# Two weight loads ahead of an activation tile in the one load ring of a fused mixer and MLP

## The chip, the cores and the metric

The kernel runs on one core of one Trainium2 chip. The metric is the device time of one execution in microseconds (us). Three runs of the kernel before gave 135.13, 135.42 and 135.43, a median of 135.42.

A core has five engines that run side by side: TensorE (PE in the profile; PEld is its weight loads), VectorE (DVE), ScalarE (ACT), GpSimd (POOL) and SyncE (SP), which here only issues DMAs. Each takes its instructions strictly in the order in which they were written for it; an instruction that waits for a semaphore holds up all that stand behind it on the same engine.

## The reference

```python
# x: 1 x 2048 x 512; w1, w2: 512 x 512; w3: 512 x 1792; w4: 1792 x 512; all bf16
def reference(x, w1, w2, w3, w4):
    B, S, D = x.shape
    h = _gelu(_layernorm(x, axis=-1) @ w1)
    c = D // 4
    g0 = jnp.pad(h[:, :, 0*c:1*c], ((0, 0), (1, 0), (0, 0)))[:, :S, :]
    g1 = jnp.pad(h[:, :, 1*c:2*c], ((0, 0), (0, 1), (0, 0)))[:, 1:, :]
    g2 = jnp.pad(h[:, :, 2*c:3*c], ((0, 0), (2, 0), (0, 0)))[:, :S, :]
    g3 = jnp.pad(h[:, :, 3*c:   ], ((0, 0), (0, 2), (0, 0)))[:, 2:, :]
    hs = jnp.concatenate([g0, g1, g2, g3], axis=-1) @ w2
    x1 = x + hs
    h2 = _gelu(_layernorm(x1, axis=-1) @ w3) @ w4
    return x1 + h2
```

The first layer normalizes each row of x, multiplies by w1, applies gelu, shifts the four quarters of the columns by +1, -1, +2 and -2 rows, multiplies by w2 and adds x. The second normalizes the rows of x1, multiplies by w3, applies gelu, multiplies by w4 and adds x1.

## The kernel before

The 2048 rows are cut into 16 tiles of 128 rows. Everything stays in SBUF: x, x1, the weights, and the transposed activations. The work is a list of named operations (`Op`), each with its engine, what it reads and writes, and an assumed duration.

Of tile t in the first layer there are, in the order of the data:

- the load of x (`dma_x...`, L384), some tiles alone, some two or three in one DMA;
- the statistics: on VectorE `bnst` (L432) and `bnag` (L434), or for the tiles in `STAT_ACT` (0, 5, 7, 9, 10, 12 in the first layer) `sum` (L411) and `ssq` (L416) on ScalarE followed by the short `msq` (L424) and `vpe` (L428) on VectorE;
- `rstd` on GpSimd (L439), a power of -0.5 that takes about 0.55 us;
- `norm`: on VectorE (L461), on ScalarE (L470) or GpSimd (L473), as `NORM` says; the last two read `nmr` (L466) as well. Tile 0 is an exception (`NAT`, `SPLIT`): `norm0_0` and `norm0_1` (L448) only subtract the mean, in two halves, and rstd0 is applied later, in gelur0;
- the transposition `tp` on TensorE (L506), copied from PSUM to SBUF by `ev` on VectorE or ScalarE (L514), `both` meaning a half on each (`ev1act` and `ev1dve`); later tiles are transposed by DMA instead (L479, issued by SP);
- the product with w1: `up1` (L642), and for tile 0 `rows0` (L544) in two halves, the first needing w1a and ev0_0, the second w1b and ev0_1; then gelu on ScalarE (L657; for tile 0 gelur0, L585). Tile 0's result is then transposed back by `th0` (L610) and copied by `evh0` on VectorE (L620);
- the product with w2, `mix` (L697), which reads the shifted columns of h of this tile and its neighbours, and `x1` on VectorE (L709, L713), which adds x.

The second layer repeats statistics, norm and transposition on x1, then `up2` (L642) with gelu (L657), `down` (L731), `res` (L739) and the store.

What sets the order:

- TensorE's order is written out by hand, in `SCRIPT`. Its beginning is `warm:9 sa:0 sb:0 ty:1 ra:0 rb:0 ty:2 up1:1 th:0 up1:2 mix:0 ty:3 mix:1`: nine matmuls of zeros (L756), tile 0 transposed in two halves, tile 1 transposed, rows0 in two halves, tile 2 transposed, up1 of tile 1, and so on.
- All loads go through one DMA ring, issued by SP in the order of the list `LOADS`. An item `w1a` is the first half of w1 (rows 0 to 255, 256 KB), `w1b` the second; `x2` is one tile (128 KB), `x0-1` two tiles in one DMA. Items `tp...` in this list only place DMA transposes among the loads; those of tiles that TensorE transposes (tile 2 among them) are ignored.
- The order on VectorE, ScalarE and GpSimd comes from the kernel's own planner when the program is built (`Program.order` and `Program.place`). It assumes a duration for every operation, a due time derived from TensorE's list, and a model of the ring; it then takes on each engine the operation that is ready and has the earliest due time (with a look ahead of 300 ns on VectorE and ScalarE). `BIAS` shifts a few due times by hand. So an edit of `LOADS` changes the assumed arrival times and may reorder any of these engines.

```python
LOADS = """
x0-1 x2 tp2 w1a w1b x3 x4-5 w2b w2a tp5 x6 tp6 x7 x8-10 tp4 w3 x12-13 tp0 x11 tp17 x14-15 tp26 tp5 w4a tp3
w4b
"""
```

`emit` writes the instructions in the planned order and adds the semaphore waits that the reads and writes need.

Of the kernel before, what the change touches and what calls it, by code (L numbers as in the profile page):

```python
# [283 lines left out]
HEV = {0: "dve", 1: "dve", 2: "dve", 3: "dve", 4: "dve", 5: "dve", 6: "dve"}  # L284
BIAS = {"bnag16": -989.166, "nmr10": 207.118, "rstd14": 756.261, "rstd5": 886.138, "ssq1": -15, "ssq15": 1115, "ssq22": -1014, "sum31": 1299.7, "x1_8": 100}
LOADS = """
x0-1 x2 tp2 w1a w1b x3 x4-5 w2b w2a tp5 x6 tp6 x7 x8-10 tp4 w3 x12-13 tp0 x11 tp17 x14-15 tp26 tp5 w4a tp3
w4b
"""
SCRIPT = """  # L290
# [618 lines left out]
```

## Time and profile before

| | |
|---|---|
| median of three runs | 135.42 us |
| span of the profiled execution, first to last instruction | 133.7 us |
| what the median has beyond that span | 1.7 us |
| TensorE busy in the span | 130.6 us (98%) |
| VectorE, ScalarE, GpSimd busy | 50.9, 56.0 and 30.9 us |
| granted TensorE clock | 1.000 |
| HBM read, written | 6.82 MB, 2.10 MB |

The profile is of one execution. Its times count from the first instruction. In the timeline a row is start, length, engine, line, operation, tiles and shapes, with the idle time of the engine before it and what ended that in square brackets. Matmuls are pipelined, and their ends are modelled: two rows that overlap by 0.16 us stand back to back, and the distance of their starts is the better measure. In the chain each row is start, length, and what the time went to. In the rows of windows the columns are the window, its length, the busy time of PE, PEld, DVE, ACT and POOL with the number of instructions, the granted clock, the share of the DMA engines and GB/s. Some matmul records are missing: where a group of four shows three and a gap of one matmul, nothing waited.

The names of single operations (bnst2, norm1, ...) are not in the profile; they follow from the order in which the operations of a line stand on their engine.

### The profile page before, as it was taken

The page shows a single profiled execution, that of the slowest core. Times are in us where ns is not written, and L with a number is a line of the kernel's source. Part 1 is how long each engine was busy: PE and PEld are TensorE (multiplying, and loading weights), DVE is VectorE, ACT ScalarE, POOL GpSimd, SP SyncE. Part 2 cuts the span into 40 slices and gives each one's busy share as a digit, 9 for nine tenths or more (in the row PEclk, how much of TensorE's full clock was granted, in tenths as well). Part 3 has the DMA queues.
Part 4 walks back from the last instruction along what each step waited for, and adds up shares of the span by engine and source line. Part 5 has one row for each costly group of instructions (what it writes and reads, how often), then busy time and mean ns, then how long its engine had stood idle before and what let it go on. Part 6 is the DMA issues. An engine that isn't in the chain of part 4 may idle for free.

```text
span 133.7 us, 2004 instructions
## 1 busy us (share of the span) xinstructions
PE 130.6 (98%) x776; PEld 71.8 (54%) x789; DVE 50.9 (38%) x138; ACT 56.0 (42%) x89; POOL 30.9 (23%) x69
## 2 busy tenths in 40 slices
PE   8999999999999999999999999999999999999994
PEld 3488768874488444444444444444444444444464
DVE  1899998887550830052260003322220000232223
ACT  5699998858657155520025553000006663000000
POOL 2447567696544120012022003100000000000000
PEclk9999999999999999999999999999999999999999
DMA  4999966745442991002211000311111000111112
GB/s 134 329 349 401 237 150 95 83 89 107 98 99 49 295 329 40 0 0 43 77 42 39 0 0 0 78 39 44 39 42 37 0 0 0 39 44 39 39 39 78
DMA packets 21305, 12.19 MB, mean 91 GB/s; under 512 B 13872, under 2 KB 20784, under 8 KB 21296
## 3 DMA queue, kind: packets, MB, share of 16 engines
q1 hardware_dynamic: 20864, 11.93, 32.7%
q10 hardware_dynamic: 432, 0.13, 0.4%
q8 instruction: 6, 0.10, 0.3%
q14 instruction: 3, 0.02, 0.1%
HBM read 6.82 MB, written 2.10 MB: 67 GB/s over the span
## 4 chain that ended last, share of the span: by engine, by line
PE 94%; DMA 2%; DVE 2%; issue 1%; SPq 0%
PE y_ps L642 46%; PE o_ps L731 36%; PE o_ps L697 10%; DMA x_sb<-in_x_dram 2%; PE y_ps L506 1%; DVE st L432 1%; PE y_ps L544 1%; DVE xn_buf L448 0%; DVE xn_buf L461 0%; DVE o_sb L739 0%; PE o_ps L610 0%; DVE mv L434 0%; SPq L894 0%
## 5 line engine op out<-in xcount | busy, mean ns | idle before, releaser
L642 PE MATMUL y_ps<-xnT,w_sb 128*128 128x512 bf16 (+2 forms) x421 | 63.6, 308 | 0.2
L642 PEld LDWEIGHTS y_ps<-xnT,w_sb 128*128 128x128 bf16 x424 | 38.4, 98 | 24.6 <-DVE mv L434 0.2
L731 PE MATMUL o_ps<-w_sb,h2T 128*128 128x512 bf16 (+3 forms) x248 | 48.7, 355 | 0.2
L657 ACT ACTIVATE h2T<-y_ps 128x1024 bf16<-128x1024 f32 (+1 forms) x29 | 28.6, 993 | 47.2 <-PE y_ps L642 47.1
L731 PEld LDWEIGHTS o_ps<-w_sb,h2T 128*128 128x128 bf16 x252 | 23.6, 98 | 25.2
L739 DVE TENSOR_TENSOR o_sb<-o_ps,x_sb 128x512 bf16<-128x512 f32 (+3 forms) x18 | 11.4, 632 | 45.7 <-PE o_ps L731 45.7
L439 POOL TENSOR_TENSOR rstd<-mv,neghalf 128x1 f32<-128x1 f32 x20 | 11.1, 553 | 35.1 <-DVE mv L434 30.1
L697 PE MATMUL o_ps<-w_sb,hT 128*128 128x512 bf16 x58 | 14.8, 379 | 0.3
L432 DVE BATCH_NORM_STATS2 st<-x_sb 128x6 f32<-128x512 bf16 x20 | 13.5, 676 | 2.6 <-DMA x_sb<-in_x_dram 2.5
L713 DVE TENSOR_TENSOR x_sb<-o_ps,x_sb 128x512 bf16<-128x512 f32 x10 | 6.8, 677 | 14.8 <-PE o_ps L697 14.8
L439 POOL TENSOR_TENSOR rstd<-vpe,neghalf 128x1 f32<-128x1 f32 x12 | 6.7, 558 | 15.6 <-DVE vpe L428 15.5
L473 POOL TENSOR_SCALAR xn_buf<-x_sb,rstd,nmr 128x512 bf16<-128x512 bf16 x12 | 9.2, 764 | 1.0 <-DVE nmr L466 0.4
L657 ACT ACTIVATE hT<-y_ps 128x512 bf16<-128x512 f32 (+1 forms) x10 | 8.1, 806 | 3.1 <-PE y_ps L642 2.9
L697 PEld LDWEIGHTS o_ps<-w_sb,hT 128*128 128x128 bf16 x64 | 6.1, 98 | 5.7
L709 DVE SCALAR_TENSOR_TENSOR x_sb<-o_ps,x_sb 128x512 bf16<-128x512 f32 x6 | 4.1, 681 | 12.1 <-PE o_ps L697 12.1
L416 ACT ACTIVATE junk<-x_sb 128x512 bf16<-128x512 bf16 x12 | 7.5, 622 | 2.1 <-DVE x_sb L709 2.0
L461 DVE TENSOR_SCALAR xn_buf<-x_sb,mv,rstd 128x512 bf16<-128x512 bf16 x13 | 6.1, 471 | 2.7 <-POOL rstd L439 2.0
L470 ACT ACTIVATE xn_buf<-x_sb,nmr,rstd 128x512 bf16<-128x512 bf16 x6 | 4.9, 813 | 0.5 <-POOL nmr L466 0.4
L756 PE MATMUL o_ps<-zeros 128*128 128x512 bf16 x9 | 4.0, 631 | 0.4 <-DVE zeros L363 0.4
L411 ACT ACTIVATE junk<-x_sb 128x512 bf16<-128x512 bf16 x6 | 3.7, 624 | 1.2 <-DMA x_sb<-in_x_dram 1.2
L434 DVE BATCH_NORM_AGGREGATE mv<-st 128x2 f32<-128x9 f32 x20 | 3.8, 192 | 0.3
L506 PE MATMUL y_ps<-ident,xn_buf 128*128 128x128 bf16 x32 | 3.4, 236 | 0.2 <-DVE xn_buf L461 0.2
(34 smaller groups left out, 28.7 us busy)
## 6 DMA issues: line engine op xcount, KB each, us to landing
out_dram<-o_sb SPq DMA_DIRECT2D x15, 128.0 KB, 1.7
w_sb<-in_w_dram SPq DMA_DIRECT2D x1, 1792.0 KB, 10.9
w_sb<-in_w_dram SPq DMA_DIRECT2D x2, 896.0 KB, 6.2
x_sb<-in_x_dram SPq DMA_DIRECT2D x4, 256.0 KB, 3.6
w_sb<-in_w_dram SPq DMA_DIRECT2D x4, 256.0 KB, 4.3
x_sb<-in_x_dram SPq DMA_DIRECT2D x5, 128.0 KB, 4.5
x_sb<-in_x_dram SPq DMA_DIRECT2D x1, 384.0 KB, 5.7
xnT<-xn_buf SPq DMA_TRANSPOSE x24, 2.5
```

Of the source, the lines that this page charges most:

```text
L416: (lambda d: (lambda e: e.activation(d, src, ACT_F.Square, accum_out=sums[:, q, 1:2])))(junk[:, b, :]),
L432: pg.add("dve", f"bnst{q}", lambda e: e.bn_stats(st9[:, q, 0:6], src), reads=rs, writes=[(("st", q), 0)], dur=605)
L439: lambda e: e.tensor_tensor(col(rstd), var, neghalf[:], ALU.pow),
L461: lambda e: e.tensor_scalar(dst, src, mv[:, q, 0:1], rstd[:, q : q + 1], ALU.subtract, ALU.mult),
L470: f = lambda e: e.activation(dst, src, ACT_F.Identity, bias=nmr[:, q : q + 1], scale=rstd[:, q : q + 1])
L473: f = lambda e: e.tensor_scalar(dst, src, rstd[:, q : q + 1], nmr[:, q : q + 1], ALU.mult, ALU.add)
L642: ins = e.matmul(y_ps[:, p, W * i : W * (i + 1)], wsb[:, dc, P * fc : P * (fc + 1)], src[:, dc, P * t0 : P * t0 + W], start=(dc == 0), sto ...
L657: (lambda d, s: (lambda e: e.activation(d, s, ACT_F.Gelu_apprx_tanh)))(dst, ysrc),
L697: ins = e.matmul(dst, hT[:, j, c0 : c0 + P], w2_sb[:, j, :], start=(j == order[0]), stop=(j == order[-1]))
L713: f = lambda e: e.tensor_tensor(x1_sb[:, t, :], dst, x_sb[:, t, :], ALU.add)
L731: ins = e.matmul(dst, h2T[:, fc, P * t : P * (t + 1)], w4_sb[:, fc, cs], start=(fc == 0), stop=(fc == FC - 1))
L739: (lambda d, c: (lambda e: e.tensor_tensor(o_sb[:, oi, c], d, x1_sb[:, t, c], ALU.add)))(dst, cs),
```

## The change

One line of the list of loads is edited:

```diff
 LOADS = """
-x0-1 x2 tp2 w1a w1b x3 x4-5 w2b w2a tp5 x6 tp6 x7 x8-10 tp4 w3 x12-13 tp0 x11 tp17 x14-15 tp26 tp5 w4a tp3
+x0-1 w1a w1b x2 tp2 x3 x4-5 w2b w2a tp5 x6 tp6 x7 x8-10 tp4 w3 x12-13 tp0 x11 tp17 x14-15 tp26 tp5 w4a tp3
 w4b
 """
```

SP thus issues x0-1, w1a, w1b, x2 and then x3 as before; the rest of its list is the same. The list and the order of TensorE are unchanged. The planner, run again on the new list, gives these orders where they differ (all operations are the same, and behind the parts shown the orders are the same as before):

```
VectorE before: zeros bnst1 bnag1 norm0_0 norm0_1 bnst2 norm1 bnag2 msq0 vpe0 norm2 ev1dve bnst3 ev2 bnag3
                bnst4 evh0 norm3 bnag4 msq5 vpe5 bnst6 norm4 bnag6 x1_0 ev4 msq7 x1_1 ev5 vpe7 bnst16
VectorE after:  zeros bnst1 bnag1 norm0_0 norm0_1 msq0 norm1 vpe0 bnst2 bnag2 ev1dve bnst3 norm2 bnag3 bnst4
                ev2 norm3 bnag4 evh0 msq5 vpe5 norm4 bnst6 bnag6 x1_0 msq7 vpe7 ev4 x1_1 ev5 bnst16
ScalarE before: gelur0 sum5 gelu1_1 ssq5 gelu1_2 sum7 ev3 norm5 ssq7 gelu1_3 sum9 ev6act norm7 gelu1_4 ssq9
                sum10 gelu1_5 ssq10 gelu1_6 sum12 ssq12
ScalarE after:  gelur0 sum5 ssq5 gelu1_1 sum7 gelu1_2 ssq7 ev3 norm5 sum9 gelu1_3 norm7 ev6act gelu1_4 ssq9
                sum10 ssq10 gelu1_5 sum12 ssq12 gelu1_6
GpSimd before:  rstd1 rstd2 rstd0 rstd3 rstd4 rstd5 nmr5 rstd6 nmr6 norm6 rstd7 nmr7
GpSimd after:   rstd1 rstd0 rstd2 rstd3 rstd4 rstd5 nmr5 rstd6 nmr6 rstd7 norm6 nmr7
```

## The prediction

> **What bounds the kernel now.** I read the chain of work that ended last first. From 5.12 us to the last store it is TensorE nearly without a break, so the question is what starts TensorE and what can stop it. The chain's window from 2.5 to 8.8 us (start, length, what):
>
> ```profile
> 0.08 2.77 DMA x_sb<-in_x_dram
> ...
> 2.87 0.70 DVE st L432
> ...
> 3.60 0.20 DVE mv L434
> 3.80 0.36 DVE xn_buf L448 x2
> 4.15 0.60 DVE st L432
> 4.75 0.33 DVE xn_buf L461
> 5.08 0.05 issue
> 5.12 0.49 PE y_ps L506 x4
> 5.62 0.86 PE y_ps L544 x4
> 6.48 0.22 PE y_ps L506 x4
> ```
>
> See: x0-1 lands, VectorE does the statistics of tile 1 (bnst1, bnag1), two halves of norm0, the statistics of tile 2 (bnst2), then norm1; that lets tp1 go (L506), behind it rows0 (L544) and tp2 (L506). The waits of TensorE from 4.6 to 131 us have one row:
>
> ```profile
> PE y_ps L506 <- DVE xn_buf L461: 0.2, 1, 0.2
> ```
>
> That is tp1 waiting for norm1. From then on TensorE waits for nothing, and in its groups the idle time is 0.2 to 0.3 us a line, in pieces of 0.05 where one matmul record is missing. So every ns that TensorE loses after 5.12 us is added to the end, and none can be gained but ahead of 5.12.
>
> Third, VectorE's and GpSimd's timelines (start, length), in which the order decides:
>
> ```profile
> 4.07 0.68 DVE L432 BATCH_NORM_STATS2 st<-x_sb 128x6 f32<-128x512 bf16 x1
> 4.67 0.39 DVE L461 TENSOR_SCALAR xn_buf<-x_sb,mv,rstd 128x512 bf16<-128x512 bf16 x1
> 4.99 0.18 DVE L434 BATCH_NORM_AGGREGATE mv<-st 128x2 f32<-128x9 f32 x1
> ...
> 5.84 0.41 DVE L461 TENSOR_SCALAR xn_buf<-x_sb,mv,rstd 128x512 bf16<-128x512 bf16 x1 [0.39 <-POOL rstd L439]
> 6.17 0.28 DVE L514 COPY xnT<-y_ps 128x256 bf16<-128x256 bf16 x1
> 6.37 0.69 DVE L432 BATCH_NORM_STATS2 st<-x_sb 128x6 f32<-128x512 bf16 x1
> ```
>
> These are bnst2, norm1, bnag2, norm2, ev1dve, bnst3. norm2 ends at 6.25 and tp2 starts at 6.32, just as rows0 is through: tile 2 arrives with nothing to spare. Hand-overs, from the rows: norm1's end (5.07) to tp1 0.06; bnag2's end (5.17) to rstd2 (5.25) 0.08; rstd2's end (5.80) to norm2 0.04; bnst1 to bnag1, which needs it, 0.03; an instruction that needs nothing starts 0.08 before its predecessor's end.
>
> Fourth, DMA by windows (last figures: share, GB/s):
>
> ```profile
> 2.50:3.00 0.50, 0.50 (x3) 0.19 (x2) 0.13 (x1) 0.13 (x1) 0.00 (x0) 1.00 0.34 94
> 3.00:3.50 0.50, 0.50 (x3) 0.23 (x2) 0.50 (x1) 0.50 (x2) 0.00 (x0) 1.00 0.61 158
> ...
> 4.00:4.50 0.50, 0.50 (x5) 0.36 (x4) 0.50 (x2) 0.21 (x2) 0.44 (x1) 1.00 1.09 379
> ```
>
> The ring runs nearly dry between x2 and w1a. Against 379 GB/s, the first two windows lose (285 + 221) x 0.5 = 253 KB, 0.67 us. By the landing events x0-1 is in at 2.85, x2 3.15, w1a 4.74, w1b 5.52, x3 5.85.
>
> **What the change removes on the path.** In the new order norm1 stands ahead of bnst2, behind norm0 and the short msq0 (0.17). rstd1 ends at 4.44 (3.88 + 0.56), so norm1 runs 4.48 to 4.87 instead of 4.67 to 5.07, and tp1 starts at 4.93: 0.19 earlier. rows0 follows it; its ev0_0 and ev0_1 end at 5.08 and 5.36, so it starts near 5.26 and is through near 6.12.
>
> w1 itself gives nothing: rows0's first half started at 5.45 with w1a in since 4.74, the second at 5.89 with w1b in since 5.52. Even 0.19 earlier the second half (5.69) would find w1b landed at the old time. TensorE, not the ring, gated w1.
>
> **What it adds on the path.** x2 now follows x0-1, w1a and w1b: the 896 KB with which w1b ended before. It lands at 5.52 if the dry stretch stays as it is, and at 5.52 - 0.67 = 4.85 if w1a's issue, 0.49 us earlier (0.59 for 1.08), lets all of it vanish. If the gap moves by exactly those 0.49, it is 5.03. I take 5.3, between this row and the upper end; both ends stay for the range.
>
> bnst2 must wait for it, and behind it VectorE's queue holds bnag2, ev1dve, bnst3, norm2, in that order: norm2 now stands behind both. Step by step:
> - bnst2 5.32 + 0.69 = 6.01; bnag2 from 6.04 to 6.23.
> - GpSimd: rstd0 now goes ahead (vpe0 is through at 4.95) and is done by 5.6; rstd2 from 6.31 to 6.86, so norm2 could start at 6.90.
> - VectorE meanwhile: ev1dve 6.15 to 6.43, bnst3 6.35 to 7.04 (x3 landed before). norm2 starts at 6.96, ends at 7.37.
> - tp2 at 7.37 + 0.06 = 7.43, against 6.32 before: **1.1 us later**. TensorE idles from 6.12 to 7.43.
>
> With x2 at 5.52 the same sum gives 7.65, or +1.3. With x2 early, bnst2 still cannot start before norm1 and vpe0 are through (4.87): it ends at 5.56, bnag2 at 5.78, ev1dve at 5.98, bnst3 at 6.59, norm2 at 6.92, tp2 at 6.98. The order alone costs **0.66**, however soon x2 lands.
>
> **What stays hidden, and what is late next.** On ScalarE ssq5 moves ahead of gelu1_1 and ssq7 ahead of ev3. gelu1_1 can't start before up1_1's end, now near 8.7; gelur0, sum5 and ssq5 (0.69 + 0.62 + 0.63 from about 6.4) are through before. From gelu1_1 to ev3 there are five instructions as before, so ev3 keeps its distance. norm7 moves ahead of ev6act, and GpSimd's rstd7 ahead of norm6, so ev6act now hangs on a chain: x1_0 ends near 11.4 (mix0 1.1 later; VectorE is free for it), msq7 and vpe7 at 11.7, rstd7 at 12.45, norm6 (0.76) at 13.3, nmr7 (0.26) at 13.7, norm7 (0.81) at 14.5, ev6act (0.38) at 14.8. up1_5, at 13.82 before, comes at 14.92: a lead of 0.1, where ev6act's end at 13.54 left 0.28. That is the next to be late; if the cover is gone it costs TensorE a few tenths, at most norm7's 0.81. evh0 comes after norm3 and bnag4: up1_2 (0.9) covers it. norm6 itself is still 0.5 ahead of tp6 (13.83). SP's transposes wait for norms that move with TensorE; tp17 had 0.8 us to up2's start and keeps it. x3 and all later loads keep their place in bytes. Nothing after 20 us changes its order; it is shifted.
>
> **One rule against the change.** The trace: the warm-up matmuls start every 0.43 us, tp0's transposes every 0.11, from about 5.4 us on every 0.06: the pace doubles 4.9 us after the first matmul, although the granted clock in the rows is 1.00 throughout. A gap before tp2 might undo this; repeating those 4.9 us at half pace would cost 2.4 us, and nothing if the pace holds. I take nothing, as the 0.45 us gap before tp1 did not keep the pace from rising. The Trainium skill ("TensorE: Matmul & The Clock Gate", Part 1) says that the clock halves after an idle window of about 3.4 us; by it a gap of 1.3 us is too short, and the sum stays. The other reading of its window, that a partly idle one counts, would make it an estimated 1.7 us (half of 3.4) longer; no row here shows which.
>
> **Sum.** The profiled span is 133.7 us; the runs' median of 135.42 has 1.7 us around it, which nothing here touches. 133.7 + 1.1 + 1.7 = **136.5 us**.
>
> **Rivals.**
> - *Order alone:* the dry stretch disappears and x2 is in by 4.9. For: w1a is issued 0.49 earlier, behind x0-1 still moving. Against: x0-1 began slowly as well (159 GB/s from 1 to 2 us), so the first bytes of a tensor may cost this wherever they stand. +0.66: 136.1.
> - *A second loss:* TensorE's pace falls in the gap, or ev6act's cover breaks as well. For: a gap of 1.3 us, a lead of 0.1. Against: the pace rose across a gap. +0.3 to +2.4 on top: 136.8 to 138.9.
> - *Absorbed (not slower):* if the 0.05 us idle pieces behind TensorE's later groups are true waits on things that come at a fixed time (w3, w4, transposes), they swallow the delay one by one; the groups show 0.2 + 0.2 + 0.3 = 0.7 us of it in all. 135.42 + 1.1 - 0.7 = 135.8, in place of a fully shifted end. It decides once at least 0.7 is given back. Against: each piece is one missing record wide.
> - *The change does what it is named for and no more:* w1 early, tile 1 earlier, tile 2 in time: -0.2, 135.2. It would need bnst2, bnag2, ev1dve, bnst3 and norm2 (2.26 us by the rows, 2.0 with the overlaps) between 4.9 and 6.26.
>
> **How the numbers follow.** Forecast 0.66, order alone 0.16, second loss 0.08, absorbed 0.07, -0.2 0.03. The range takes x2 from 4.85 to 5.52 (136.1 to 136.7) and the runs' own spread (135.13 to 135.43), and reaches a little to the absorbed and the second-loss cases: 135.8 to 137.1. A measurement of this kernel tells about 0.3%, 0.4 us: faster by more 0.02, within 0.08, slower by more 0.90.
>
> **What would show it.** Right: tp1 near 4.9; bnst2 waiting for the DMA of x_sb until 5.0 to 5.5; tp2 between 7.0 and 7.7 behind an idle TensorE that the waits put down to norm2 (L461); afterwards no other wait, span about 134.8. Wrong: tp2 before 6.9, a further wait of TensorE after 8 us, or starts 0.11 apart after tp2.

## The result and the profile after

The changed kernel took 136.25 us (three runs, 136.16 to 136.58) against 135.42 (135.13 to 135.43): ratio 1.0062, 95% interval 1.0035 to 1.0089. It is slower by 0.83 us. Its profiled execution took 136.25 with a span of 134.9, 1.2 more than the span before. Medians in this document are of all executions of a kernel; ratios and their intervals leave out executions more than 1.5% above the kernel's fastest.

TensorE's waits from 4.6 to 131 us, by the view of waits (who waited, for whom, us in total, times, longest):

```profile
PE y_ps L506 <- DVE xn_buf L461: 0.5, 1, 0.5
PE o_ps L697 <- ACT hT L657: 0.2, 1, 0.2
```

The first is tp2 waiting for norm2, as forecast. The second, mix1 waiting for gelu1_2, was not forecast. VectorE's timeline shows the first (start, length):

```profile
4.27 0.41 DVE L461 TENSOR_SCALAR xn_buf<-x_sb,mv,rstd 128x512 bf16<-128x512 bf16 x1 [0.20 <-POOL rstd L439]
...
5.04 0.69 DVE L432 BATCH_NORM_STATS2 st<-x_sb 128x6 f32<-128x512 bf16 x1 [0.29 <-DMA x_sb<-in_x_dram]
5.77 0.20 DVE L434 BATCH_NORM_AGGREGATE mv<-st 128x2 f32<-128x9 f32 x1
...
6.65 0.40 DVE L461 TENSOR_SCALAR xn_buf<-x_sb,mv,rstd 128x512 bf16<-128x512 bf16 x1
```

norm1 runs early; bnst2 waits for x2, which lands at 5.02 (before: 3.15); norm2 ends at 7.04. TensorE's timeline:

```profile
5.23 1.42 PE L544 MATMUL y_ps<-w_sb,xnT 128*128 128x512 bf16 x4
7.10 0.40 PE L506 MATMUL y_ps<-ident,xn_buf 128*128 128x128 bf16 x4 [0.45 <-DVE xn_buf L461]
...
10.21 0.39 PE L506 MATMUL y_ps<-ident,xn_buf 128*128 128x128 bf16 x4
10.82 1.04 PE L697 MATMUL o_ps<-w_sb,hT 128*128 128x512 bf16 x4 [0.22 <-ACT hT L657]
```

tp2 starts at 7.10 instead of 6.32, 0.78 late. tp3 (10.21) takes 0.22, so mix1 could have started at 10.43; it starts at 10.82, 0.39 late. 0.78 + 0.39 is the 1.2 of the span. (The bracket counts to a matmul's modelled end, so it shows less than what TensorE loses.) ScalarE's timeline tells where the 0.39 comes from:

```profile
8.56 0.58 ACT L657 ACTIVATE hT<-y_ps 128x512 bf16<-128x512 f32 x1
9.55 0.63 ACT L411 ACTIVATE junk<-x_sb 128x512 bf16<-128x512 bf16 x1 [0.41 <-DMA x_sb<-in_x_dram]
...
10.18 0.58 ACT L657 ACTIVATE hT<-y_ps 128x512 bf16<-128x512 f32 x1
```

These are gelu1_1, sum7 and gelu1_2. sum7 now stands ahead of gelu1_2 and waits for the landing of x7, at 9.53 here (9.09 in the profile before). In the ring, the dry stretch is gone (last figures: share, GB/s):

```profile
2.50:3.00 0.50, 0.50 (x3) 0.19 (x2) 0.33 (x1) 0.33 (x1) 0.00 (x0) 1.00 1.02 324
3.00:3.50 0.50, 0.50 (x3) 0.22 (x2) 0.47 (x2) 0.50 (x3) 0.00 (x0) 1.00 1.01 332
```

They moved 94 and 158 before. x2 lands half a us ahead of the 5.52 at which w1b had ended the same 896 KB. That is less than the 0.67 us lost in the dry stretch, and from 4.5 to 5.5 the ring now moves less (231 and 195 GB/s, against 371 and 342 before).

### The profile page after: what moved, and what is told of

It reads as the page before. It is cut to its first block, busy times and chain, and to the rows that moved or that the text cites. A ratio compares the mean times of both kernels' runs of the same rounds, so it can differ in the third digit from the quotient of the medians.

```text
span 134.9 us, 2016 instructions
## 1 busy us (share of the span) xinstructions
PE 132.0 (98%) x789; PEld 71.9 (53%) x789; DVE 51.3 (38%) x138; ACT 56.1 (42%) x89; POOL 31.1 (23%) x69
## 4 chain that ended last, share of the span: by engine, by line
PE 91%; DMA 4%; SPq 2%; ACT 1%; issue 0%; DVE 0%
PE y_ps L642 44%; PE o_ps L731 36%; PE o_ps L697 10%; DMA x_sb<-in_x_dram 4%; SPq L384 1%; SPq L393 1%; PE y_ps L506 1%; ACT junk L411 1%; ACT hT L657 0%; DVE o_sb L739 0%
## 5 line engine op out<-in xcount | busy, mean ns | idle before, releaser
L697 PE MATMUL o_ps<-w_sb,hT 128*128 128x512 bf16 x64 | 15.8, 379 | 0.2 <-ACT hT L657 0.2
```

The lines of the kernel that those rows point to most:

```text
L697: ins = e.matmul(dst, hT[:, j, c0 : c0 + P], w2_sb[:, j, :], start=(j == order[0]), stop=(j == order[-1]))
```

## The experiments

The theory after the result: (a) TensorE loses what tp2 is late, and tp2 follows x2's landing; (b) it loses again at mix1 where sum7 waits for x7; (c) the planner's new orders cost 0.66 by themselves, however early x2 is. Rivals: only the orders cost; only the ring costs; the pace of TensorE, not its waits, makes the difference.

Moves were made by a function that, after planning, puts a named operation behind another on the same engine (`MOVE`) and leaves all else in place. The runs below the first two rows were measured in three groups of four, each beside its own runs of the kernel before (medians 135.51, 135.59 and 135.49); the first group ran on another chip than the second and third. The table has, from each profile, the landings of x2 and x7 by the landing events, the starts of tp2 and mix1 and the span, then the median and its ratio to the kernel before. "Half pace" marks a start that can't be compared, since TensorE's granted clock had fallen to 0.50 for 3.41 us.

| run | x2 | x7 | tp2 | mix1 | span | median | ratio |
|---|---|---|---|---|---|---|---|
| before | 3.15 | 9.09 | 6.32 | 9.64 | 133.7 | 135.42 | |
| after | 5.02 | 9.53 | 7.10 | 10.82 | 134.9 | 136.25 | 1.0062 (1.0035 to 1.0089) |
| ring_only | 5.82 | 9.38 | half pace | | 137.1 | 138.42 | 1.0192 (1.0152 to 1.0233) |
| orders_only | 3.25 | 9.91 | 7.92 | 11.25 | 135.3 | 136.20 | 1.0057 (1.0036 to 1.0077) |
| sum7_behind | 6.39 | 9.57 | 8.47 | half pace | 137.9 | 137.32 | 1.0128 (1.0108 to 1.0148) |
| x2_behind_x3 | 6.59 | 10.15 | 8.68 | half pace | 137.7 | 137.00 | 1.0111 (1.0091 to 1.0130) |
| before_again | 3.32 | 9.84 | 6.98 | 10.30 | 134.4 | 135.42 | 0.9986 (0.9967 to 1.0005) |
| after_again | 5.62 | 9.97 | 7.70 | 11.25 | 135.4 | 136.84 | 1.0080 (1.0052 to 1.0107) |
| after_fill | 5.95 | 9.54 | 8.03 | 11.36 | 135.4 | 136.78 | 1.0087 (1.0064 to 1.0111) |
| x2_mid | 4.86 | 9.55 | 7.20 | 10.83 | 134.9 | 136.25 | 1.0054 (1.0033 to 1.0074) |
| ring_only_fill | 6.19 | 9.68 | 8.47 | 11.80 | 135.9 | 136.66 | 1.0086 (1.0065 to 1.0108) |
| before_fill | 3.24 | 9.24 | 6.37 | 9.69 | 133.8 | 135.41 | 0.9991 (0.9978 to 1.0004) |
| act_as_before | 5.36 | 8.69 | 7.44 | 10.77 | 135.6 | 137.08 | 1.0120 (1.0100 to 1.0139) |
| after_third | 6.02 | 9.46 | 8.10 | half pace | 137.1 | 136.55 | 1.0074 (1.0053 to 1.0095) |

**Ring alone, orders alone.** ring_only is the kernel before with

```diff
+MOVE = [('dma_x2', 'dma_w1b')]
```

> The new order of the load ring (x0-1, w1a, w1b, x2) with every engine's order as before the change. Theory (the late x2 is what costs; the planner's new orders only share it out): bnst2 stands ahead of norm1 and waits for x2 until 5.0, norm1 ends near 6.0, tp1 starts near 6.1, norm2 ends near 7.2, tp2 starts near 7.3 instead of 6.32; gelu1_2 stands ahead of sum7 again, so no wait of TensorE behind mix0. Span 133.7 + 1.0 = 134.7. Rival (the new orders cost, not the ring): TensorE meets x2 in time or nearly, span 133.7 to 133.9.

tp1 started at 6.91 (expected 6.1: x2 landed at 5.82, not 5.0), and then came what neither theory had: TensorE ran at half pace for 3.4 us. Five of its six executions took 138.3 to 140.0, one 136.73. Four of the five have a mean granted clock of 0.988, which is what one such stretch makes of the span; the fifth and longest (139.97) has 1.000, so what held it is not known. So the new ring alone is worse than the whole change: with the old order bnst2 stands ahead of norm1, and the late x2 holds tp1 as well. Without the half pace (ring_only_fill below, 1.0086) it is no worse than the whole change (1.0074 beside it): what the planner's new order repairs is the long gap ahead of tp1.

orders_only is the changed kernel with `MOVE = [('dma_x2', 'dma_x0')]`, which puts x2 back to its place behind x0-1.

> The engines' orders as after the change, with the load ring as before (x2 second, landing near 3.2). Theory: the orders alone cost some 0.66, because bnag2, ev1dve and bnst3 stand ahead of norm2: tp2 near 7.0, x7 lands near 9.1 so that sum7 holds up gelu1_2 and mix1 by less than 0.1; span 134.4. Rival (only x2's landing costs): tp2 near 6.3 to 6.5, span 133.7 to 133.9.

The price of the orders is there: 0.57%, 0.77 us by the times, where 0.66 was expected. Its profile, of the slowest of its six executions, shows more: tp2 at 7.92 and not near 7.0, since the loads behind x2 landed late in this execution. TensorE's timeline:

```profile
5.27 0.61 PE L544 MATMUL y_ps<-w_sb,xnT 128*128 128x512 bf16 x2
6.52 0.61 PE L544 MATMUL y_ps<-w_sb,xnT 128*128 128x512 bf16 x2 [0.64 <-DMA w_sb<-in_w_dram]
7.92 0.40 PE L506 MATMUL y_ps<-ident,xn_buf 128*128 128x128 bf16 x4 [0.79 <-DVE xn_buf L461]
```

Here w1b, in its old place, lands at 6.47 and holds the second half of rows0 (by the starts, 6.52 in place of 5.72, so by 0.8). Then tp2 waits for norm2, which stands behind bnst3, and that waits for x3, as VectorE's timeline has it:

```profile
6.86 0.69 DVE L432 BATCH_NORM_STATS2 st<-x_sb 128x6 f32<-128x512 bf16 x1 [0.81 <-DMA x_sb<-in_x_dram]
7.47 0.40 DVE L461 TENSOR_SCALAR xn_buf<-x_sb,mv,rstd 128x512 bf16<-128x512 bf16 x1
```

So norm2's place behind bnst3 costs more than its length: tile 2 then waits for tile 3's load.

Either half alone costs about as much as the whole change, so the two don't add: the orders alone 0.57%, the ring alone (ring_only_fill) 0.86%, both together 0.62 to 0.80%. In the first profile of the changed kernel tp2 stands at 7.10, and 6.98 was the forecast for the orders alone, so there x2 adds little to them. How late x2 is matters beyond that floor, as the next runs show.

**The place of x2, as a dose.** x2_behind_x3 is the changed kernel with `MOVE = [('dma_x2', 'dma_x3')]`; x2_mid has `MOVE = [('dma_w1b', 'dma_x2')]`, which gives x0-1, w1a, x2, w1b.

> The changed kernel with x2 one place later still (x0-1, w1a, w1b, x3, x2), engine orders as after the change. Theory: x2 lands where x3 did, near 5.9 instead of 5.0, so tp2 moves by the same 0.86 to near 8.0; the wait of mix1 for gelu1_2, which ends at a fixed time set by the landing of x7, is swallowed by the delay: net 0.86 - 0.38 = 0.5, span 135.4. Rival (waits add up): span 135.8. Rival (the landing of x2 isn't what holds norm2): 134.9.

> The changed kernel with x2 between w1a and w1b in the ring; engine orders as after the change. Theory: x2 lands 256 KB earlier, 0.7 to 1.0, so tp2 falls by as much until the floor of the orders alone (tp2 near 7.0) is met: 0.1 to 1.0 faster than after_again in the same call. If w1b then lands after 5.9 it holds rows0's second half, which is hidden while norm2 is later still. Rival (x2's place in the ring matters little): as after_again.

With the new orders tp2 follows x2 exactly: 5.02 to 7.10, 5.36 to 7.44, 5.62 to 7.70, 5.95 to 8.03, 6.02 to 8.10, 6.39 to 8.47 and 6.59 to 8.68 are all 2.08 or 2.09 apart. x2_mid meets the floor: 4.86 to 7.20, where bnst2 starts as VectorE comes free and bnst3 waits a little for x3. Its median is 0.5 below that of after_again beside it, without the latter's one execution at half pace, but the intervals overlap. The ends of the scale are clear: with the same orders, x2 second (orders_only) has 1.0057 and x2 behind x3 1.0111, measured together. That the waits swallow each other could not be read from x2_behind_x3's times, since its profile has half pace; the law below shows it in the others.

**The second wait.** sum7_behind is the changed kernel with `MOVE = [('sum7', 'gelu1_2_0')]`. act_as_before moves all of ScalarE's operations back to their order before:

```diff
+MOVE = [('ssq5', 'gelu1_1_0'), ('sum7', 'gelu1_2_0'), ('ssq7', 'norm5'), ('sum9', 'gelu1_3_0'), ('norm7', 'ev6act'), ('ssq10', 'gelu1_5_0'), ('gelu1_6_0', 'ssq10')]
```

> The changed kernel with one move on ScalarE: sum7 behind gelu1_2, as before the change. Theory (two waits add up, 0.78 at tp2 for norm2 and 0.38 at mix1, whose gelu1_2 stands behind sum7, which waits for the landing of x7 near 9.5): the second wait goes, tp2 stays near 7.1, span 134.9 - 0.4 = 134.5. Rival (the 0.38 is TensorE's own or another operation's): span 134.9 as the changed kernel.

> The changed kernel with ScalarE's whole order as before the change (sum7 behind gelu1_2, ssq7 behind norm5, norm7 behind ev6act), the rest as after. Theory: mix1 starts at the later of tp2 + 3.33 and, where sum7 stands ahead of gelu1_2, the landing of x7 + 1.28 (10.81 for x7 at 9.53, 11.25 for 9.97, 10.83 for 9.55). Here only the first is left: 0.2 to 0.4 faster than after_third in the same call, and no wait of TensorE after tp2. Rival (x7 holds TensorE by another way, at ev3 as in sum7_behind): as after_third, with the wait at up1_3.

In every profile at full pace with sum7 ahead of gelu1_2, mix1 starts at the later of tp2 + 3.33 and x7 + 1.28: after 10.82 (10.43 and 10.81), after_again 11.25 (11.03 and 11.25), x2_mid 10.83 (10.53 and 10.83), after_fill 11.36 (11.36 and 10.82), orders_only 11.25 (11.25 and 11.19). The second term comes with sum7's place: in before_again, where sum7 stands behind gelu1_2, x7 landed as late as 9.84, yet mix1 started at 10.30 = 6.98 + 3.32, not at 11.12. act_as_before can't show it: mix1 starts at 10.77 = 7.44 + 3.33, but x7 had landed at 8.69 in this execution and would not have held mix1 in either order. The gain I expected did not come; it is slower than after_third (1.0120 against 1.0074). Its waits:

```profile
PE y_ps L506 <- DVE xn_buf L461: 1.4, 2, 1.2
PE y_ps L642 <- DVE xnT L514: 0.4, 1, 0.4
```

The new one is up1_4 waiting for ev4. VectorE's timeline (vpe7, then ev4):

```profile
12.99 0.16 DVE L428 SCALAR_TENSOR_TENSOR vpe<-sums,mv 128x1 f32<-128x1 f32 x1 [0.91 <-ACT junk L416]
13.07 0.42 DVE L514 COPY xnT<-y_ps 128x512 bf16<-128x512 bf16 x1
```

In the planner's new order VectorE has vpe7 ahead of ev4, which is right only if ScalarE has done ssq7 early. With ssq7 back behind norm5, VectorE stands 0.91 us in front of vpe7 with ev4 behind it. The late vpe7 also delays rstd7, and behind it on GpSimd norm6, for which the next transposition (tp6) waits. The orders belong together; half of one plan was worse than the whole of either. sum7_behind missed as well: it is slower than the changed kernel (1.0128), where 0.4 us less was expected. It says nothing of the second wait: with x2 at 6.39 there was none to remove, and its profile has half pace. It has a wait of 0.2 at up1_3 for ev3, as sum7 and ssq7 then both stand between gelu1_2 and ev3. So (b) is shown as a law of the start of mix1, and in the profile by ScalarE's wait for x7; that its removal alone would bring its 0.2 to 0.4 us is not shown.

**The pace.** after_fill adds five matmuls of zeros between rows0 and tp2, ring_only_fill six between tp0 and tp1, before_fill one there; the planner is told that they take no time, so that its orders stay.

```diff
-warm:9 sa:0 sb:0 ty:1 ra:0 rb:0 ty:2 up1:1 th:0 up1:2 mix:0 ty:3 mix:1 ty:4 up1:3 ty:5 up1:4 ty:6 mix:2
+warm:9 sa:0 sb:0 ty:1 ra:0 rb:0 warm:5 ty:2 up1:1 th:0 up1:2 mix:0 ty:3 mix:1 ty:4 up1:3 ty:5 up1:4 ty:6 mix:2
```

> The changed kernel with five more matmuls of zeros on TensorE between rows0 and tp2 (about 1.1 us at full pace), where it idles for norm2; they are no part of the result. Theory (idling lets the pace fall): no execution shows half pace after tp2, and the time is that of the undisturbed executions of after_again, or 0 to 0.4 more where x2 lands early and the added matmuls end after norm2. Rival (the pace has other causes): as many executions at half pace as in after_again.

> ring_only (new ring, orders as before) with six more matmuls of zeros on TensorE between tp0 and tp1, where it idled 2.4 us for norm1; they are no part of the result. Theory (TensorE's idle time lets the pace fall): half pace after tp1 is gone, which 5 of ring_only's 6 executions seem to have had (138.3 to 140.0 beside one of 136.7); time 136.5 to 137.0, the spread below 1 us. Rival (the half pace comes from something else, such as the late w1 or the chip): 138.4 as ring_only, most executions above 138.

> The kernel before with one more matmul of zeros on TensorE between tp0 and tp1, in its 0.45 to 0.6 us of idle time there; no part of the result. In before_again rows0 ran at half pace (starts 0.43 apart until 6.5), in the first profile from 5.4 us on at full pace, and tp2 started 0.66 later. Theory (the pace rises after a stretch in which TensorE was never idle): the rise comes earlier or as early in every execution, 0 to 0.4 faster than before, less spread. Rival (when it rises is chance, or tied to the first matmul): same time as before, or some 0.1 more where the added matmul holds tp1.

In ring_only's windows (first busy figure PE, then PEld, DVE, ACT, POOL; before the last two the granted clock):

```profile
3.97:7.38 3.41, 1.05 (x12) 0.60 (x11) 1.60 (x7) 0.99 (x5) 0.87 (x2) 1.00 0.92 289
7.38:10.79 3.41, 3.41 (x25) 2.58 (x24) 2.31 (x6) 1.64 (x4) 1.27 (x3) 0.50 1.04 373
10.80:14.20 3.40, 3.35 (x40) 2.45 (x39) 2.68 (x9) 3.23 (x8) 1.87 (x5) 1.00 1.02 407
```

and in ring_only_fill's:

```profile
2.95:6.36 3.41, 3.41 (x12) 1.44 (x11) 1.35 (x5) 1.95 (x6) 0.62 (x1) 1.00 1.00 285
6.37:9.77 3.40, 3.10 (x35) 1.93 (x34) 2.98 (x11) 1.51 (x4) 1.13 (x3) 1.00 1.00 335
```

A stretch of 3.41 us with TensorE busy for 1.05 is followed by one at 0.50; a full one is not. With the fill all six executions took 136.31 to 137.24 at a granted clock of 1.000, though x2 landed later than in ring_only's profile, and the span is what the waits alone give: 133.7 + (8.47 - 6.32) = 135.9. So the idle time causes the half pace, as far as two kernels measured at different times on different chips can show it; that it isn't the first chip alone follows from after_again and after_third, which had half pace on the second. after_fill points the same way but can't settle it alone: no half pace in six executions, where after_again had one in seven. before_fill made no difference that can be measured; its spread is no smaller either (135.07 to 135.66, against 135.08 to 135.71 beside it), so its theory is not borne out. In its profile the pace had risen before the added matmul (tp0 at 4.15 takes 0.39 us, against 0.63 in the first profile), so that execution tests nothing.

**Repeats.**

> The kernel before, unchanged, for a profile beside the others. Theory (the loads land by up to a us later in some executions, whatever the ring's order): w1b between 5.5 and 6.5; TensorE is held at rows0's second half only if w1b lands after 5.9; span 133.7 to 134.3. Rival (the later landings of the last profiles come from the changed orders): w1b at 5.5 as in the first profile, x3 at 5.9.

> The changed kernel, unchanged. Theory: tp2 starts 2.08 after x2 lands (5.02 and 7.10 in its first profile, 6.39 and 8.47 in that of sum7_behind); span 133.7 + (tp2 - 6.32) + the wait at mix1 for gelu1_2, which is 0.4 where tp2 is at 7.1 and 0 where it is over 7.6; with x2 between 5.0 and 6.4 the span is 134.9 to 135.9. Where TensorE idles for some 2 us, some executions run the next 3 us at half pace, 1.6 to 2 us more. Rival (the first profile was the rule): x2 at 5.0, tp2 at 7.1, time 136.2.

> The changed kernel, unchanged, as the measure for act_as_before on the same chip. Theory: tp2 2.08 after x2's landing, mix1 at the later of tp2 + 3.33 and x7 + 1.28; 136.2 to 136.9, 0.6 to 1.0% above before. Rival: none; it is a repeat.

The landings of one and the same ring differ by a us between executions: w1b in the old ring at 5.52, 5.88, 6.47 and 6.49; x2 in the new ring at 5.02 to 6.39. That is what the theory of before_again said, not its rival; and w1b, landing after 5.9 there, did hold rows0's second half, as it said. tp2 starts 0.66 later there than in the first profile. TensorE's timeline of before_again (its lines count one higher):

```profile
5.28 0.61 PE L507 MATMUL y_ps<-ident,xn_buf 128*128 128x128 bf16 x4 [0.39 <-DVE xn_buf L462]
5.68 1.46 PE L545 MATMUL y_ps<-w_sb,xnT 128*128 128x512 bf16 x4
6.98 0.39 PE L507 MATMUL y_ps<-ident,xn_buf 128*128 128x128 bf16 x4
```

and, of its weight loads, those of rows0's second half:

```profile
6.53 0.11 PEld L545 LDWEIGHTS y_ps<-w_sb,xnT 128*128 128x128 bf16 x2 [0.70 <-DMA w_sb<-in_w_dram]
```

rows0 takes 1.3 us to tp2's start, not 0.86. Its four matmuls start at 5.68, 6.11, 6.54 and 6.76. Three things add up. x0-1 landed 0.16 later. The pace rose only near 6.2, against 5.4 in the first profile, so tp1 and rows0's first half ran slowly: about 0.3. And the second half waited for w1b, which landed at 6.49: at full pace from 6.2 it would have started near 6.36, so this is an estimated 0.2. The view of matmul waits misses it, since the matmul before it is modelled as busy until then; the row of the weight loads shows it. before_fill's second half waited too, by the same kind of row, for the w1b of 5.88 (0.1 by the starts). In the new kernel the same slow rows0 (5.23 to near 6.5 in its first profile) is hidden, as TensorE waits for norm2 anyway.

after_third's profile caught half pace, after TensorE had idled 1.8 us for norm2:

```profile
4.95:8.36 3.41, 1.52 (x13) 0.73 (x14) 2.39 (x9) 2.62 (x7) 1.24 (x3) 1.00 1.04 340
8.36:11.77 3.41, 3.41 (x36) 3.41 (x34) 2.17 (x9) 1.41 (x5) 1.25 (x3) 0.50 1.06 396
```

Of the 16 executions of the changed kernel two went so (138.48 and 138.89); the other 14 took 136.08 to 137.01.

For all profiles at full pace the span is 133.7, plus what tp2 is later than 6.32, plus what mix1 waits: after_again 133.7 + 1.38 + 0.22 = 135.3 (measured 135.4), orders_only 133.7 + 1.60 = 135.3 (135.3), x2_mid 133.7 + 0.88 + 0.30 = 134.9 (134.9), before_again 133.7 + 0.66 = 134.4 (134.4). Only act_as_before has a further term, near 0.75: by the starts, up1_4 is 0.57 late behind ev4 and tp6 another 0.18 behind norm6.

## Why the prediction was right, and where it was not

- *What bounds it:* right. Every ns that TensorE loses behind 5 us is in the span, by the sums above.
- *x2's place is the price:* right. tp2 was forecast 2.13 behind the landing of x2; it is 2.08. The forecast took x2 at 5.3 between 4.85 and 5.52; it was 5.02 in the first profile, hence 0.78 for the forecast 1.1 (only about 0.1 of it above the 0.66 of the orders), but 5.36 to 6.39 in the other profiles with this ring. The upper end was mis-sized: it was taken from one execution of the kernel before, in which w1b landed earliest of all that were seen.
- *The order alone costs 0.66:* right in kind, and near in size, in part by luck. orders_only is slower by 0.77 us with x2 in at its old time, and x2_mid's tp2 stands at 7.20, near the 6.98 of the sum. But the forecast took x3 as landed; bnst3 ties norm2 to x3's landing, and in the one profile of orders_only that wait is part of the price.
- *w1 gives nothing:* right for the execution profiled first, wrong as a rule. In the three other profiles with the old ring rows0's second half waited for w1b: 0.8 us by the starts in orders_only, an estimated 0.2 in before_again, 0.1 in before_fill. The early w1 is worth something where the loads are late, and less than the late x2 costs.
- *ScalarE's moves are hidden:* wrong. The step counted the instructions between gelu1_1 and ev3 and found them equal in number; it did not ask what the one that came between gelu1_1 and gelu1_2 waits for. sum7 waits for x7: 0.39 us in the first profile. By the prediction's own sign (a further wait of TensorE after 8 us) this part of it is refuted. The cover expected to be thin, ev6act's, held: it ended at 14.74, 0.28 ahead of up1_5.
- *The pace:* nothing was taken, and that held for the median. The second loss was real and of about the forecast size, but it came in 2 of 16 executions. Of the two readings of the window named there, the runs bear out the other one: a partly idle window sufficed.
- *The sum:* 1.1 on the median of 135.42 gave 136.5; 136.25 was measured, inside the range. That the span came out at 134.9 for a forecast of 134.8 is luck, two misses that cancel: tp2 0.3 less late, mix1 0.4 more. And what lies around the span is 1.35 (136.25 - 134.9; 135.73 - 134.4 in before_again), not 1.7: the profiled execution before was a short one. A median execution before has a span near 134.1, which is why the medians differ by 0.8 and the two spans by 1.2.

No run points to a version that beats the kernel before.

## What to carry to other kernels

A transfer that is moved up in a ring moves others down: ask first which of the two the busy engine meets sooner, and then follow each instruction that the planner moved to the load that it waits for, not only to the engine that it runs on. Price a late load as a law (arrival plus the chain behind it) and take its arrival from several executions, since it differed here by a us. Orders that one plan made for two engines go together; taking back one of them was worse here than either.

## What the runs showed of the hardware

TensorE's pace changes on a grid of 3.41 us that lies differently in each execution: the granted clock fell to 0.50 for one such stretch after one in which TensorE was busy for 1.05 us (ring_only), 1.24 (x2_behind_x3), 1.52 (after_third) or 1.61 (sum7_behind). It stayed at 1.00 after one of 2.96 (after) and after one of 2.56 (x2_behind_x3, 3.06 to 6.48). In these four profiles an idle time of 1.8 to 2.4 us was enough. Most other executions of the last three kernels show no half pace; their gaps were not profiled. The Trainium skill ("TensorE: Matmul & The Clock Gate", Part 1) describes a free-running window of 3413 ns, which agrees, and names an idle window as the condition; here a half idle one sufficed.

The first rise of the pace belongs to the same grid: in ring_only it came near 4.0 us (tp0 at 4.15 already takes 0.39), and the fall at 7.38. In two executions of the kernel before it came at 5.4 and near 6.2, and the later rise cost the second about 0.3 of its 0.66 us.
